# A spectral filter branch beside a split-fp16 feed-forward branch: first products and subtractions reordered, third quarter's rows in a place of their own, unit stores on GpSimd sooner, filter loaded for two quarters at a time

## The chip, the cores and the metric

One core of one Trainium2 chip. The metric is the device time of one execution in microseconds (us). The kernel before the change took 1266.6 us, the median of three runs (1266.14 to 1267.13).

## The reference

x has 2048 rows of 1024. Its rows are normalised, and two branches work on the result: a two-dimensional real Fourier transform, multiplied by a complex filter and transformed back, and a feed-forward network with hidden width 3584.

```python
def _A_ref(x, w_r, w_i):
    X = jnp.fft.rfft2(x, axes=(-2, -1))
    X = X * (w_r + 1j * w_i)
    return jnp.fft.irfft2(X, s=(S, D), axes=(-2, -1))

def _B_ref(x, w1, w2):
    h = _silu(jnp.einsum("bsd,df->bsf", x, w1))
    return jnp.einsum("bsf,fd->bsd", h, w2)

xn = _layernorm(x, axis=-1)
s = _A_ref(xn, A_w_r, A_w_i)
g = _silu(_B_ref(xn, B_w1, B_w2))
return x + s * g
```

## The kernel before

Every number of a product is held as a high and a low fp16 part, so that one product of 128x512 is three matmuls (high by high, high by low, low by high). DVE makes the low parts (`low`, L271, and L961 for the rows), ACT the high parts (`high`, L268, and L957).

**Order.** Nothing here is ordered by a scheduler. The kernel issues every engine's instructions itself: TensorE's products are a list, and behind each product a function (the one that ends with the loop over `bg` near L1705) takes a step of background work from the queues `bg` (normalisation, Fourier work), `wq` (weights), `xq`, `yq` and `sq` (sums of weights). Each piece is a generator, and a `yield` ends its step. A model of the clock decides how far DVE's work may run ahead of TensorE's (`LEAD`, 2.5 us). `defer(n, ...)` puts a load or store n steps later. Each engine takes its instructions strictly in the order issued, and an instruction that waits holds up all behind it. SP, ACT and POOL issue DMAs from the same order as their other work.

**Start.** The rows come in four quarters c of 512 rows, each of four row tiles p. `load_x` loads one row tile, `ln_gen(c)` normalises it: statistics on DVE (L936 to L939), the scale on POOL (L941 to L943), the normalisation on ACT (L944), and for c = 0 and 1 transposes on TensorE (`tp`, L953), whose results ACT and DVE split (L957, L961). Quarters 2 and 3 go through `turned`: ACT normalises into `xp` and writes the high part of `xs` (L922), DVE the low part (L915), and SP transposes both by DMA (L908). The row tiles of all quarters share four places; a row tile of the next quarter is loaded when its place comes free. `mm1(c, f)` is one product pa{c}_{f} of 24 matmuls (L618) for the hidden tile f of w1; DVE finds each w1 tile's scale (L303, L275 to L278). `spin` matmuls (L1716), counted by `WARM`, keep TensorE at work before the first product. fa0 to fa3 (L1017 to L1019) are the first Fourier stage; `AT` says behind which product of quarter 1 the first two of them stand. Each finished pair of hidden tiles gives sums and differences, split and stored to DRAM as "units" of seven blocks (`hosum`, `hoone`; stores at L702): the first two units through SP's queue, all others through POOL's.

**Middle.** Strassen-like products for the first half of the hidden width (L656), then the second matrix product in blocks pb{m}_{j} of 42 matmuls (L784 to L786), whose left operands `w<-hd` ACT's queue loads back from DRAM (L741), five steps ahead. w2's blocks, r, are loaded by SP (L556), some have a second block added by an accumulating DMA from POOL's queue (L561), and are split by ACT (L268) and DVE (L271).

**Filter stage.** Woven into that, `f_gen` goes through 16 units u: a second Fourier stage on TensorE (`fx`, L1234 to L1236) from vq (`load_v`, L1212), a radix-4 step on DVE that gives X (to L258), the multiplication by the filter (L1312, L1313), four sums into Z (L1341 to L1344), and the split of Z (ACT L1263, DVE L1273), of which each four units are stored to zd by POOL (L1256, the last high part from a tile called fs). `load_w(u)` loads the filter's real and imaginary parts for one unit, 128x4x128 fp32 each (L1220), and ACT scales them (L1298). `part_of(u)` gives unit u's group q and its column block j; for j = 0 POOL copies a column of X (L1294). X, T2 (the second product) and Z take turns in three places.

**Edge.** The column at the half frequency is worked out by `edge_gen` in small steps: copies on POOL (L1368 to L1371), nine small matmuls (eps, L1375 to L1377), ACT's copy (L1380), some thirty operations of 128x16 on POOL (L1385), a scaling (L1421), then ACT and DVE write zp (L1424, L1425). Its first step is taken in unit 13.

**Inverse.** `i_gen` reads zd back (SP, L1483), POOL copies a column of zp into it (L1574), and TensorE does the inverse transforms (iu L1499, id L1528).

Of the kernel before, what the change touches and what calls it, by code (L numbers as in the profile page):

```python
# [21 lines left out]
WARM = [35, 8, 0, 8, 0, 8, 12, 0, 0, 0]  # L22
# [8 lines left out]
AT = (1, 0)  # L31
# [111 lines left out]
def spectral_ffn(ctx, tc, x, w_r, w_i, w1, w2, ca, kc, ci, tw, pm, out):  # L143
# [467 lines left out]
    def mm1(c, f):  # L611
        ps = pf.tile([128, 512], F32, name=f"pa{c}_{f}", tag="ff")
        w, xt = w1t[f], xnT[c]
        terms = [(d, wh, xh) for wh, xh in ((0, 0), (0, 1), (1, 0)) for d in range(8)]
        if c + f:
            terms.sort(key=lambda k: k[0])
        for n, (d, wh, xh) in enumerate(terms):
            nc.tensor.matmul(ps, w[:, wh, d], xt[:, xh, d], start=(n == 0), stop=(n == 23))  # L618
        if c == 3:
            used1.add(f)  # L620
            done1.pop(f)()
        q, g = f // 2, c // 2

        def evac():
            if (q, g) not in h32:
                h32[q, g] = H["h"].tile([128, 4, 512], F32, name=f"h32_{q}_{g}", tag="h32", bufs=2)
            hq = h32[q, g]
            nc.scalar.activation(hq[:, 2 * (c % 2) + f % 2], ps, AF.Silu, scale=ep[:, q:q + 1])  # L628
            if c % 2 and f % 2:
                return hidden(q, g)  # L630

        return evac
# [259 lines left out]
    def load_x(c, p):  # L892
        tag, bufs = ("Ro", 1) if (c, p) == (0, 3) else ("x", 4)
        t_ = A["p"].tile([128, 1024], F32, name=f"x{c}_{p}", tag=tag, bufs=bufs)
        nc.sync.dma_start(t_, xs[4 * c + p])
        A["x"][c, p] = t_
# [4 lines left out]
    def turned(c, stats, norm):  # L901
# [9 lines left out]
        for i in range(4):  # L911
            if i >= 2:
                for p in (2 * i - 4, 2 * i - 3):
                    turn(p, 0)
                    nc.vector.tensor_tensor(split[:, p, 1], xn[p], split[:, p, 0], op=OP.subtract)  # L915
                    turn(p, 1)
            if i in (1, 2):
                for p in (2 * i - 2, 2 * i - 1):
                    xn[p] = ap.tile([128, 8, 128], F32, name=f"xp{c}_{p}", tag="Rs", bufs=2)
                    norm[p](xn[p].rearrange("s d1 d0 -> s d0 d1"), A["x"][c, p].rearrange("s (d0 d1) -> s d0 d1", d1=8))  # L920
                    A["x"].pop((c, p))
                    nc.scalar.activation(split[:, p, 0], xn[p], AF.Copy)  # L922
                    if c < 3:
                        defer(1, lambda p=p: load_x(c + 1, p))
            if i < 2:
                for p in (2 * i, 2 * i + 1):
                    stats(p)
            yield 2.5

    def ln_gen(c):  # L930
# [33 lines left out]
        if c == 0:  # L964
# [18 lines left out]
            hi(3)  # L983
            yield 0
            lo(2)
# [6 lines left out]
        for i in range(4):  # L992
            pair = range(2 * (i % 2), 2 * (i % 2) + 2)
            for p in pair:
                if i < 2:
                    stats(p)
                else:
                    trans(p)
                    if c < 3:
                        load_x(c + 1, p)  # L1000
# [187 lines left out]
    def open_f():  # L1188
        spots = {"K": (32, 38), "vq": (44, 48), "xc": (28,), "xb": (30,), "xd": (62,), "T1": (24,), "zl": (8,)}
        spots = {k: [(X1, v * KB) for v in vs] for k, vs in spots.items()}  # L1190
        spots["w"] = [(X1, 52 * KB + 2064 * k) for k in range(4)]
        spots["X"] = [(X1, 16 * KB), (X1, 20 * KB), (R2[0], 60 * KB)]
# [5 lines left out]
        load_w(1)  # L1198

    def part_of(u):  # L1200
        return u // 4, (u % 4 if u < 12 else (u - 1) % 4)
# [13 lines left out]
    def load_w(u):  # L1215
        q, j = part_of(u)
        n = 129 if j == 3 else 128
        for i in range(2):
            t_ = B["p"].tile([128, 4, n], F32, name=f"wq{u}_{i}", tag="w", bufs=4)
            nc.sync.dma_start(t_, wv[i][q][:, :, 128 * j:128 * j + n])  # L1220
            B["w"][u, i] = t_

    def f_gen():
# [21 lines left out]
        load_v(1)  # L1245
        yield PAUSE
# [33 lines left out]
        for u in range(16):  # L1280
# [9 lines left out]
            X = bp.tile([128, 8, 128], F32, name=f"X{u}", tag="X", bufs=3)  # L1290
# [4 lines left out]
            w_ = [B["w"].pop((u, i)) for i in range(2)]  # L1295
            for i in range(2):
                wf = w_[i].rearrange("m a k -> m (a k)")
                nc.scalar.activation(wf, wf, AF.Copy, scale=zs)  # L1298
                if j in (0, 3):
                    at = 0 if j == 0 else 128  # L1300
                    nc.scalar.activation(xsv[:, 1 + j // 3, q, :, i:i + 1], w_[i][:, :, at:at + 1], AF.Copy)
# [7 lines left out]
            wr, wi = (t_[:, :, 0:128].unsqueeze(2).broadcast_to([128, 4, 2, 128]) for t_ in w_)  # L1309
            t1 = bp.tile([128, 4, 2, 128], F32, name=f"T1{u}", tag="T1", bufs=1)  # L1310
            t2 = bp.tile([128, 4, 2, 128], F32, name=f"T2{u}", tag="X", bufs=3)
            tt(t1, Xv, wr, op=OP.mult)  # L1312
            tt(t2, Xv, wi, op=OP.mult)  # L1313
            if u + 2 < 16:
                defer(2, lambda u=u: load_w(u + 2))
# [4 lines left out]
            if u >= 13:  # L1320
# [11 lines left out]
            if u >= 14:  # L1332
# [4 lines left out]
            Z = bp.tile([128, 8, 8, 16], F32, name=f"Z{u}", tag="X", bufs=3)  # L1337
# [131 lines left out]
    def open_r2():  # L1469
        R2[0] = A["r2"].enter_context(tc.tile_pool(name="r2", bufs=1, side="right")).tile([128, 19520], F32, name="r2")  # L1470
# [199 lines left out]
    with tc.manual_schedule():  # L1670
# [27 lines left out]
        def work():  # L1698
# [5 lines left out]
            for _ in range(3):  # L1704
                if clock["dve"] > clock["pe"] + LEAD or hold[0] or slot(bg) == PAUSE:  # L1705
# [25 lines left out]
        for k, q in enumerate((bg, wq, bg, wq, bg, wq, wq, bg, wq)):  # L1731
            slot(q)
            spin(WARM[1 + k])
        for i in range(4):
            load_x(1, i)
            if i == 1:
                load_fwd()
        for c in range(1, 4):
# [5 lines left out]
        order = [(c, f) for fs in ((0, 1, 2, 3), (4, 5)) for c in range(2) for f in fs]  # L1744
        order += [(c, f + i) for f in (0, 2, 4) for c in (2, 3) for i in range(2)]
        order += [(c, f + i) for f in range(6, 2 * NPL, 2) for c in range(4) for i in range(2)]
        t_job = None
        for n, (c, f) in enumerate(order):
            if f == 0 and c:
                finish(bg, ln[c])  # L1750
            if ln[3].done and stores[0] is nc.sync:
                stores[0] = nc.gpsimd
# [167 lines left out]
```

## Time and profile before

| | |
|---|---|
| Median of three runs | 1266.6 us |
| The profiled execution, its own time | 1267.57 us |
| Its span in the profile | 1265.8 us |
| Mean granted TensorE clock | 0.995 |
| Busy: PE, DVE, ACT, POOL | 1232.4, 991.6, 567.0, 272.5 us |
| DMA | 306.68 MB, mean 242 GB/s |

The span leaves out 1.77 us around it. All times below that have a start are microseconds from the span's start. "<-" behind a wait names what ended it; a row "x16" stands for 16 instructions one behind the other, with the time that they took together.

### The profile page before, as it was taken

The numbers are of one execution on the slowest core, as the hardware profiler recorded it, in microseconds if no ns is written. First come the engines' busy times: TensorE is split into PE (matmuls) and PEld (weight loads), VectorE is DVE, ScalarE is ACT, GpSimd is POOL, SyncE is SP. The second block draws the span as 40 slices with busy tenths as digits, with TensorE's granted clock in tenths as the row PEclk, the third lists the DMA queues.
The fourth block names the chain that finished last, engine by engine and source line by source line (L and its number), as shares of the span: only waits on it lengthen the run. The fifth ranks groups of instructions, "written<-read, shape, count | busy, mean of one in ns | idle before, by whom it ended". The sixth has DMA issues, their size and how long they took to land. (4 is left out here: it accounts for less than half of the span.)

```text
span 1265.8 us, 18607 instructions
## 1 busy us (share of the span) xinstructions
PE 1232.4 (97%) x6827; PEld 639.3 (51%) x6827; DVE 991.6 (78%) x1646; ACT 567.0 (45%) x844; POOL 272.5 (22%) x428
## 2 busy tenths in 40 slices
PE   8999999999999999999999999999999989999998
PEld 5544444444444444444545455555554446666654
DVE  6677998889996977897587869996799238977875
ACT  4755465755457777766423223232333113412221
POOL 1321243433242313342200000202121400110111
PEclk9999999999999999999999999999999999999999
DMA  7469697767569878866956788989999998987687
GB/s 235 127 155 234 159 305 220 221 185 220 118 186 254 245 241 281 247 194 217 333 152 201 243 253 212 314 251 279 221 299 290 320 344 281 341 279 277 220 268 270
DMA packets 184187, 306.68 MB, mean 242 GB/s; under 512 B 32032, under 2 KB 92448, under 8 KB 182944
## 3 DMA queue, kind: packets, MB, share of 16 engines
q1 hardware_dynamic: 138176, 163.85, 42.8%
q0 software_dynamic: 30128, 92.82, 25.5%
q10 hardware_dynamic: 15792, 48.83, 10.9%
q8 instruction: 53, 0.87, 0.3%
q14 instruction: 38, 0.31, 0.1%
HBM read 204.25 MB, written 111.67 MB: 250 GB/s over the span
## 5 line engine op out<-in xcount | busy, mean ns | idle before, releaser
L618 PE MATMUL pa<-xn,w 128*128 128x512 f16 x1536 | 335.5, 380 | 6.8 <-DMA xn<-xs 2.4
L784 PE MATMUL pb<-r,w 128*128 128x512 f16 (+1 forms) x798 | 299.5, 375 | 1.7 <-DMA w<-hd_one 1.7
L785 PE MATMUL pb<-r,w 128*128 128x512 f16 (+1 forms) x798 | 299.5, 375 | 0.0
L786 PE MATMUL pb<-r,w 128*128 128x512 f16 (+1 forms) x798 | 299.5, 375 | 0.0
L618 PEld LDWEIGHTS <-w 128*128 128x128 f16 x1536 | 150.2, 98 | 188.1 <-issue 4.2
L656 PEld LDWEIGHTS <-w 128*128 128x128 f16 x1008 | 98.5, 98 | 124.8 <-issue 5.5
L786 PEld LDWEIGHTS <-w 128*128 128x128 f16 x798 | 78.1, 98 | 91.2
L784 PEld LDWEIGHTS <-w 128*128 128x128 f16 x798 | 78.1, 98 | 88.3 <-DMA w<-hd_one 3.2
L785 PEld LDWEIGHTS <-w 128*128 128x128 f16 x798 | 78.1, 98 | 85.0
L656 PE MATMUL pa<-r,w 128*128 128x512 f16 x432 | 99.1, 379 | 4.8 <-ACT pc L668 2.6
L268 ACT ACTIVATE r<-r,sc 128x512 f16<-128x512 f32 x88 | 61.1, 715 | 93.0 <-DMA r<-in_B_w_dram 66.0
L271 DVE SCALAR_TENSOR_TENSOR r<-r,sc 128x512 f16<-128x512 f32 x88 | 65.0, 747 | 38.0 <-ACT r L268 38.0
L702 POOL DMA_DIRECT2D hd_one<-hoone x52 | 45.7, 879 | 178.2 <-DVE hoone L271 158.2
L271 DVE SCALAR_TENSOR_TENSOR hoone<-h,hs,hoone 128x2048 f16<-128x2048 f32 x28 | 65.7, 2346 | 8.1 <-ACT hoone L268 7.9
L268 ACT ACTIVATE hoone<-h,hs 128x2048 f16<-128x2048 f32 x28 | 55.8, 1994 | 14.1 <-DMA hd_one<-hoone 8.0
L702 POOL DMA_DIRECT2D hd_sum_d<-hosum x26 | 23.6, 907 | 165.3 <-DVE hosum L271 107.9
L268 ACT ACTIVATE hosum<-hr,hs 128x1536 f16<-128x1536 f32 x28 | 43.9, 1568 | 34.1 <-DVE hr L709 23.4
L271 DVE SCALAR_TENSOR_TENSOR hosum<-hr,hs,hosum 128x1536 f16<-128x1536 f32 x28 | 50.7, 1812 | 9.3 <-ACT hosum L268 9.3
L628 ACT ACTIVATE h<-pa,ep 128x512 f32<-128x512 f32 x64 | 43.2, 677 | 32.7 <-PE pa L618 30.7
L1499 PE MATMUL iu<-xn 128*128 128x256 f16 x384 | 44.6, 273 | 4.7 <-POOL xn L1574 2.6
L1234 PE MATMUL fx<-xn 128*128 128x256 f16 x192 | 44.8, 279 | 4.0 <-DVE r L271 2.9
L708 DVE TENSOR_TENSOR hr<-h 128x1024 f32<-128x1024 f32 x28 | 34.2, 1220 | 14.3 <-ACT h L628 13.1
(292 smaller groups left out, 2060.2 us busy)
## 6 DMA issues: line engine op xcount, KB each, us to landing
w<-hd_dif ACTq DMA_DIRECT2D x32, 448.0 KB, 7.0
r<-in_B_w_dram SPq DMA_DIRECT2D x56, 256.0 KB, 8.0
w<-hd_sum ACTq DMA_DIRECT2D x32, 448.0 KB, 6.6
w<-hd_one ACTq DMA_DIRECT2D x32, 448.0 KB, 7.3
hd_sum<-hosum POOLq DMA_DIRECT2D x52, 256.0 KB, 6.0
hd_one<-hoone POOLq DMA_DIRECT2D x52, 256.0 KB, 4.7
hd_dif<-hoone POOLq DMA_DIRECT2D x52, 256.0 KB, 4.4
xn<-in_B_w_dram SPq DMA_DIRECT2D x40, 256.0 KB, 4.9
```

Source lines behind the costliest of these rows:

```text
L268: nc.scalar.activation(hi, raw, AF.Copy, scale=scale)
L271: nc.vector.scalar_tensor_tensor(lo, raw, scale, hi, op0=OP.mult, op1=OP.subtract)
L618: nc.tensor.matmul(ps, w[:, wh, d], xt[:, xh, d], start=(n == 0), stop=(n == 23))
L628: nc.scalar.activation(hq[:, 2 * (c % 2) + f % 2], ps, AF.Silu, scale=ep[:, q:q + 1])
L656: nc.tensor.matmul(ps, lhs(d, wh), rhs(d, xh), start=(name in ("M1", "M5") and d + n == 0), stop=(d + n == 5), skip_group_check=True)
L702: defer(1, lambda k=k, m=m: stores[0].dma_start(hd[m, g][:, :, q].rearrange("f p h s -> f p (h s)"), o[:, k].rearrange("f p h s -> f p (h ...
L708: tt(sums[:, 0:2], hq[:, 0::2], hq[:, 1::2], op=OP.subtract)
L784: nc.tensor.matmul(ps, hh[:, 0], w[:, 0], start=first, stop=False)
L785: nc.tensor.matmul(ps, hh[:, 0], w[:, 1], start=False, stop=False)
L786: nc.tensor.matmul(ps, hh[:, 1], w[:, 0], start=False, stop=last)
L1234: nc.tensor.matmul(o, k[:, c, kh, 1], v[:, c, vh], start=(n == 0), stop=False)
L1499: nc.tensor.matmul(ps[:, q], lhs, rhs, start=(n == 0 and r == 0), stop=(n == 2 and r == 1))
```

## The change

Seven things are edited.

1. In `ln_gen(0)` the third row tile's subtraction is issued one step sooner, two slots of the start change places, and `WARM` changes with them.
2. `mm1` for c >= 1 takes its terms in the order high-high, low weight, low row; pa1_0 takes them one whole group behind the other. pa1_0 goes ahead of fa0_0 and fa0_1 (`AT`), and pa1_4 ahead of pa0_5.
3. The row tiles of quarter 2 get places of their own and are loaded at the start, behind those of quarter 1; those of quarter 3 are loaded from `ln_gen(1)`.
4. `LEAD` is 6 between the issue of w1's sixth tile and the end of quarter 3's normalisation.
5. The units' stores go to POOL's queue from the second step of quarter 3's normalisation on, so that all units go there.
6. `load_w(t)` loads the filter for two units at once, 128x4x256 (or 257), in four places; ACT scales them at once. T2 overwrites X, X and Z take turns in two places. Units 12 to 15 take the column blocks 0, 1, 3, 2 instead of 3, 0, 1, 2.
7. `edge_gen`'s first step is taken in unit 14, a second one per unit from unit 15.

```diff
 NP = NFT // 2
-WARM = [35, 8, 0, 8, 0, 8, 12, 0, 0, 0]
+WARM = [35, 8, 0, 8, 0, 2, 16, 0, 0, 0]
 LEAD, PAUSE, EARLY = 2.5, -1, 2
...
 TURNED = (2, 3)
-AT = (1, 0)
+AT = (1, 1)
 EXTRA = (4, 5, 6, 7, 20, 22, 24)
...
         w, xt = w1t[f], xnT[c]
-        terms = [(d, wh, xh) for wh, xh in ((0, 0), (0, 1), (1, 0)) for d in range(8)]
-        if c + f:
+        terms = [(d, wh, xh) for wh, xh in (((0, 0), (1, 0), (0, 1)) if c else ((0, 0), (0, 1), (1, 0))) for d in range(8)]
+        if (c, f) not in ((0, 0), (1, 0)):
             terms.sort(key=lambda k: k[0])
...
         tag, bufs = ("Ro", 1) if (c, p) == (0, 3) else ("x", 4)
-        t_ = A["p"].tile([128, 1024], F32, name=f"x{c}_{p}", tag=tag, bufs=bufs)
+        if c == 2:
+            t_ = view(X1, 48 * KB + 4 * KB * p, [128, 1024], F32)
+        else:
+            t_ = A["p"].tile([128, 1024], F32, name=f"x{c}_{p}", tag=tag, bufs=bufs)
         nc.sync.dma_start(t_, xs[4 * c + p])
...
                     nc.scalar.activation(split[:, p, 0], xn[p], AF.Copy)
-                    if c < 3:
-                        defer(1, lambda p=p: load_x(c + 1, p))
             if i < 2:
...
                     stats(p)
+            if c == 3 and i == 1:
+                stores[0] = nc.gpsimd
             yield 2.5
...
             hi(3)
-            yield 0
             lo(2)
+            yield 0
             lo(3)
...
                     trans(p)
-                    if c < 3:
-                        load_x(c + 1, p)
+                    load_x(3, p)
             if i < 2:
...
         spots = {k: [(X1, v * KB) for v in vs] for k, vs in spots.items()}
-        spots["w"] = [(X1, 52 * KB + 2064 * k) for k in range(4)]
-        spots["X"] = [(X1, 16 * KB), (X1, 20 * KB), (R2[0], 60 * KB)]
+        spots["w"] = [(X1, 52 * KB), (X1, 56 * KB), (R2[0], 60 * KB), (R2[0], 72 * KB + 256)]
+        spots["X"] = [(X1, 16 * KB), (X1, 20 * KB)]
         spots["zh"] = [(X1, 0), (H["scr"], 0)]
...
         load_w(0)
-        load_w(1)
 
     def part_of(u):
-        return u // 4, (u % 4 if u < 12 else (u - 1) % 4)
+        return u // 4, (u % 4 if u < 12 else (0, 1, 3, 2)[u % 4])
 
...
 
-    def load_w(u):
-        q, j = part_of(u)
-        n = 129 if j == 3 else 128
+    def load_w(t):
+        q, j = t // 2, 2 * (t % 2)
+        n = 257 if j else 256
         for i in range(2):
-            t_ = B["p"].tile([128, 4, n], F32, name=f"wq{u}_{i}", tag="w", bufs=4)
+            t_ = B["p"].tile([128, 4, n], F32, name=f"wq{t}_{i}", tag="w", bufs=4)
             nc.sync.dma_start(t_, wv[i][q][:, :, 128 * j:128 * j + n])
-            B["w"][u, i] = t_
+            B["w"][t, i] = t_
 
...
         load_v(1)
+        load_w(1)
         yield PAUSE
...
             tt(d.rearrange("m c r k -> m c (r k)"), pv[:, 0:2], cpy, op=OP.subtract)
-            X = bp.tile([128, 8, 128], F32, name=f"X{u}", tag="X", bufs=3)
+            X = bp.tile([128, 8, 128], F32, name=f"X{u}", tag="X", bufs=2)
             radix4(-1, b, d, X)
...
                 nc.gpsimd.tensor_copy(xsv[:, 0, q], Xv[:, :, :, 0])
-            w_ = [B["w"].pop((u, i)) for i in range(2)]
-            for i in range(2):
+            w_ = [B["w"][u // 2, i] for i in range(2)]
+            for i in range(2 if u % 2 == 0 else 0):
                 wf = w_[i].rearrange("m a k -> m (a k)")
                 nc.scalar.activation(wf, wf, AF.Copy, scale=zs)
-                if j in (0, 3):
-                    at = 0 if j == 0 else 128
-                    nc.scalar.activation(xsv[:, 1 + j // 3, q, :, i:i + 1], w_[i][:, :, at:at + 1], AF.Copy)
+                at = 256 if u % 4 else 0
+                nc.scalar.activation(xsv[:, 2 if at else 1, q, :, i:i + 1], w_[i][:, :, at:at + 1], AF.Copy)
             yield 2.8
...
                 high_z(u - 1)
-            wr, wi = (t_[:, :, 0:128].unsqueeze(2).broadcast_to([128, 4, 2, 128]) for t_ in w_)
+            wr, wi = (t_[:, :, 128 * (j % 2):128 * (j % 2) + 128].unsqueeze(2).broadcast_to([128, 4, 2, 128]) for t_ in w_)
             t1 = bp.tile([128, 4, 2, 128], F32, name=f"T1{u}", tag="T1", bufs=1)
-            t2 = bp.tile([128, 4, 2, 128], F32, name=f"T2{u}", tag="X", bufs=3)
+            t2 = Xv
             tt(t1, Xv, wr, op=OP.mult)
             tt(t2, Xv, wi, op=OP.mult)
-            if u + 2 < 16:
-                defer(2, lambda u=u: load_w(u + 2))
+            if u % 2 and u < 13:
+                defer(2, lambda u=u: load_w(u // 2 + 2))
             if u == 12:
...
                 edge = edge_gen()
-            if u >= 13:
+            if u >= 14:
                 next(edge, None)
...
                 low_z(u - 1)
-            if u >= 14:
+            if u >= 15:
                 next(edge, None)
...
                 copy(u + 1)
-            Z = bp.tile([128, 8, 8, 16], F32, name=f"Z{u}", tag="X", bufs=3)
+            Z = bp.tile([128, 8, 8, 16], F32, name=f"Z{u}", tag="X", bufs=2)
             bv = b2.rearrange("m a r (i l) -> m a r l i", l=8)
...
             for _ in range(3):
-                if clock["dve"] > clock["pe"] + LEAD or hold[0] or slot(bg) == PAUSE:
+                if clock["dve"] > clock["pe"] + (LEAD if ln[3].done or 5 not in w1t else 6) or hold[0] or slot(bg) == PAUSE:
                     break
...
         spin(WARM[0])
-        for k, q in enumerate((bg, wq, bg, wq, bg, wq, wq, bg, wq)):
+        for k, q in enumerate((bg, wq, bg, wq, bg, wq, bg, wq, wq)):
             slot(q)
...
                 load_fwd()
+        for i in range(4):
+            load_x(2, i)
         for c in range(1, 4):
...
 
-        order = [(c, f) for fs in ((0, 1, 2, 3), (4, 5)) for c in range(2) for f in fs]
+        order = [(c, f) for c in range(2) for f in range(4)] + [(c, f) for f in (4, 5) for c in range(2)]
         order += [(c, f + i) for f in (0, 2, 4) for c in (2, 3) for i in range(2)]
         order += [(c, f + i) for f in range(6, 2 * NPL, 2) for c in range(4) for i in range(2)]
-        t_job = None
+        t_job = sum_job = None
         for n, (c, f) in enumerate(order):
...
                 finish(bg, ln[c])
-            if ln[3].done and stores[0] is nc.sync:
-                stores[0] = nc.gpsimd
+            if ln[3].done and not sum_job:
                 sum_job = add(sq, sum_gen())
```

In the following rows a name such as w_67 is a tile that is used again and again, tp_2 is the transposed third row tile, and r_, xn stand for big regions. From the row loads (L894) on, the kernel after has its lines shifted by one to three.

DVE at the start, before, from the first w1 tile's second maximum on (L303 maxima, L275 to L278 its scale, L961 low parts of the rows, L271 low parts of w1):

```order
L303 TENSOR_REDUCE m_221<-w_67 128x1
L275 TENSOR_SCALAR ep<-s_0_402 128x1
L276 TENSOR_SCALAR ep<-ep 128x1
L277 RECIPROCAL rs_225<-ep 128x1
L278 TENSOR_SCALAR hs<-rs_225 128x1
L271 SCALAR_TENSOR_TENSOR w_67<-w_67,rs_225 128x1024
L961 TENSOR_TENSOR xn<-tp_2_362,xn 128x8x128
L961 TENSOR_TENSOR xn<-tp_3_383,xn 128x8x128
L271 SCALAR_TENSOR_TENSOR w_67<-w_67,rs_225 128x1024
```

The same stretch after (L964 is the former L961):

```order
L303 TENSOR_REDUCE m_221<-w_67 128x1
L964 TENSOR_TENSOR xn<-tp_2_362,xn 128x8x128
L275 TENSOR_SCALAR ep<-s_0_397 128x1
L276 TENSOR_SCALAR ep<-ep 128x1
L277 RECIPROCAL rs_225<-ep 128x1
L278 TENSOR_SCALAR hs<-rs_225 128x1
L964 TENSOR_TENSOR xn<-tp_3_383,xn 128x8x128
L271 SCALAR_TENSOR_TENSOR w_67<-w_67,rs_225 128x1024 x2
```

One of the two low parts now stands ahead of the scale, the other ahead of the first of w1's low parts.

POOL at the end of the filter stage, before (L1385 "ISA" stands ahead of the edge's operations; L561 accumulating loads of w2, L1256 stores of zd):

```order
L561 DMA r_2501<-in_B_w_dram 128x512 x7
L1385 ISA
L1385 TENSOR_TENSOR xn<-xsv,xn 128x16 x3
L1385 TENSOR_TENSOR xn<-xn,xsv 128x16
L1385 TENSOR_TENSOR xn<-xsv,xn 128x16 x4
L1385 TENSOR_TENSOR xn<-xn 128x16 x14
L561 DMA r_2501<-in_B_w_dram 128x512 x4
L1256 DMA zd<-fs 128x4096
L561 DMA r_2501<-in_B_w_dram 128x512
L1256 DMA zd<-xn 128x4096
L1385 TENSOR_TENSOR xn<-xn 128x16 x2
L1385 TENSOR_TENSOR xn<-xn 128x4 x8
```

And after (L1258 and L1386 are the former L1256 and L1385):

```order
L561 DMA r_2496<-in_B_w_dram 128x512 x10
L1258 DMA zd<-fs 128x4096
L561 DMA r_2496<-in_B_w_dram 128x512
L1258 DMA zd<-xn 128x4096
L1386 ISA
L1386 TENSOR_TENSOR xn<-xsv,xn 128x16 x3
L1386 TENSOR_TENSOR xn<-xn,xsv 128x16
L1386 TENSOR_TENSOR xn<-xsv,xn 128x16 x4
L1386 TENSOR_TENSOR xn<-xn 128x16 x16
L1386 TENSOR_TENSOR xn<-xn 128x4 x8
L1422 TENSOR_SCALAR xn<-xn 128x32
```

The whole edge now stands behind the last accumulating load and both stores of zd.

ACT at the same place, before (L741 loads of w from hd, L865 an activation of a finished block):

```order
L268 ACTIVATE r_2501<-r_2501,sc_229 128x512
L741 DMA w_67<-hd_one_1_94 128x1792
L268 ACTIVATE r_2501<-r_2501,sc_229 128x512
L1424 ACTIVATE zp<-xn 128x16x2
L741 DMA w_67<-hd_one_1_94 128x1792
L865 ACTIVATE pl_2_1_8559<-pl_2_1_8559,c_228 128x512
L268 ACTIVATE r_2501<-r_2501,sc_229 128x512 x2
L741 DMA w_67<-hd_one_1_94 128x1792 x2
L865 ACTIVATE pl_3_1_8632<-pl_3_1_8632,c_228 128x512
```

And after (L1425 is the former L1424):

```order
L268 ACTIVATE r_2496<-r_2496,sc_229 128x512
L741 DMA w_67<-hd_one_1_94 128x1792
L268 ACTIVATE r_2496<-r_2496,sc_229 128x512
L741 DMA w_67<-hd_one_1_94 128x1792
L865 ACTIVATE pl_2_1_8499<-pl_2_1_8499,c_228 128x512
L268 ACTIVATE r_2496<-r_2496,sc_229 128x512
L1425 ACTIVATE zp<-xn 128x16x2
L268 ACTIVATE r_2496<-r_2496,sc_229 128x512
L741 DMA w_67<-hd_one_1_94 128x1792 x2
L865 ACTIVATE pl_3_1_8572<-pl_3_1_8572,c_228 128x512
```

ACT's write of zp now stands behind one more load of w and ahead of the next two.

On TensorE the products keep their order but for pa1_0 and pa1_4 (above); the edge's nine matmuls stood ahead of pb4_0 and now stand behind pb4_1.

More of the change, by code (lines that the diff above doesn't have):

```diff
@@ L1469, in open_r2 @@
     def open_r2():
[L1470 removed]
+        R2[0] = A["r2"].enter_context(tc.tile_pool(name="r2", bufs=1, side="right")).tile([128, 19524], F32, name="r2")
     def open_fd():
```

2 lines of the change are left out of this document (1 added, 1 removed).

## The prediction

> **What bounds the kernel now.** I read the page first, then TensorE's waits, then a table of stretches, then the timelines of the engines that those waits name. The page's first lines:
>
> ```profile
> span 1265.8 us, 18607 instructions
> PE 1232.4 (97%) x6827; PEld 639.3 (51%) x6827; DVE 991.6 (78%) x1646; ACT 567.0 (45%) x844; POOL 272.5 (22%) x428
> ```
>
> TensorE is busy 97% of the span: only 1265.8 - 1232.4 = 33 us can be won by fewer waits, besides what the clock loses. The change takes 2 spin matmuls away and no product. So each part is judged by the waits it touches. TensorE's waits (line, what it waited for, us in all, times, longest):
>
> ```profile
> PE iu L1499 <- POOL xn L1574: 2.6, 1, 2.6
> PE pa L618 <- DMA xn<-xs: 2.4, 2, 1.3
> PE pa L618 <- DVE w L271: 2.2, 1, 2.2
> PE pb L784 <- DMA w<-hd_one: 1.7, 3, 1.3
> PE pa L618 <- DVE xn L961: 1.7, 1, 1.7
> PE fa L1017 <- DVE xn L961: 1.5, 1, 1.5
> ```
>
> These six, 12.1 us, lie where the change works; two more, of fx, stand below. Behind some waits the granted clock also fell. The stretches (length, then PE's, PEld's, DVE's, ACT's, POOL's busy time, granted clock, DMA share, GB/s):
>
> ```profile
> 100.00:120.00 20.00, 17.61 (x74) 7.38 (x73) 17.49 (x30) 11.12 (x12) 0.20 (x1) 0.91 0.90 223
> 890.00:925.00 35.00, 30.95 (x195) 17.34 (x193) 27.41 (x48) 10.39 (x22) 3.42 (x4) 0.95 0.98 259
> 1000.00:1046.00 46.00, 39.54 (x228) 21.51 (x226) 15.59 (x28) 9.51 (x14) 0.26 (x1) 1.00 0.95 347
> ```
>
> Work at 0.91 for 17.61 us loses 1.6, at 0.95 for 30.95 us loses 1.5. From 890 to 925 and from 1000 to 1046 the DMA engines are 95% busy and more: a load there waits for others.
>
> **Start.** DVE, TensorE's first product behind it, and ACT's last high rows of quarter 1:
>
> ```profile
> 17.72 0.16 DVE L275 TENSOR_SCALAR ep<-s 128x1 int32<-128x1 int32 x1 [1.40 <-PE s L283]
> 19.48 1.28 DVE L271 SCALAR_TENSOR_TENSOR w<-w,rs 128x1024 f16<-128x1024 f32 x1 [1.03 <-ACT w L268]
> 20.69 2.35 DVE L961 TENSOR_TENSOR xn<-tp,xn 128x1024 f16<-128x1024 f32 x2
> 23.09 3.61 PE L618 MATMUL pa<-xn,w 128*128 128x512 f16 x16 [1.68 <-DVE xn L961]
> 45.30 1.94 ACT L957 ACTIVATE xn<-tp 128x1024 f16<-128x1024 f32 x2 [3.30 <-PE tp L953]
> ```
>
> Each L961 takes 2.35/2 = 1.18. The first fits into the 1.40 that DVE waits ahead of the scale, the second nearly into the 1.03 ahead of L271. The low rows are then there about 20, before TensorE's first eight matmuls end: -1.7. pa1_0 begins with high rows only, where fa waited 1.5 for low ones. ACT has the high ones at 47.24, DVE's last low ones take another half of a pair's 2.35 or less: between nothing and -1.1, I take -0.4. So TensorE is 2.1 ahead when it comes to pa0_4, and there a new wait opens:
>
> ```profile
> 65.39 1.23 DVE L915 TENSOR_TENSOR xs<-xp,xs 128x1024 f16<-128x1024 f32 x1 [1.93 <-ACT xs L922]
> 70.04 1.28 DVE L271 SCALAR_TENSOR_TENSOR w<-w,rs 128x1024 f16<-128x1024 f32 x1
> 50.31 26.50 PE L618 MATMUL pa<-xn,w 128*128 128x512 f16 x122
> 79.02 15.28 PE L618 MATMUL pa<-xn,w 128*128 128x512 f16 x70 [2.21 <-DVE w L271]
> ```
>
> A matmul is 26.50/122 = 0.217. pa0_4 is the fifth product from 50.31: its third matmul, the first with w_4's low part, stood at 50.31 + 98 x 0.217 = 71.6, and that part was ready at 71.3. Coming 2.1 earlier it waits up to 1.8. DVE's chain to it begins with a wait for ACT's xs, which the earlier rows shorten; I grant 0.3 and take +1.5. pa0_5's 2.2 goes, because pa1_4 (24 x 0.217 = 5.2 us) now stands ahead of it: -2.2. Next, quarter 3's rows (first row ACT, second SP):
>
> ```profile
> 94.73 2.00 ACT L268 ACTIVATE hoone<-h,hs 128x2048 f16<-128x2048 f32 x1 [5.36 <-DMA hd_one<-hoone]
> 94.65 12.12 SPq L908 DMA_TRANSPOSE xn<-xs  x8
> ```
>
> ACT waited 5.36 for the first unit's store before it could go on to quarter 3's third row tile, and SP's eight transposes stretched over 12.12 us behind ACT and DVE. In the new order xp and xs stand ahead of that hoone, and SP has no unit stores between: I expect the last transpose some us ahead of TensorE, so -2.4 for its two waits and -1.6 for the clock. What comes next is the copy of pa1_4's result on ACT, now behind the xs work and a hoone whose store is on POOL:
>
> ```profile
> L702 POOL DMA_DIRECT2D hd_one<-hoone x52 | 45.7, 879 | 178.2 <-DVE hoone L271 158.2
> ```
>
> POOL's stores take 0.88 us each to issue, seven of them 6.2, so TensorE may wait for a bank; I bound that by nothing and half of it, 3.1, and take 1.2. Start: -1.7 - 0.4 + 1.5 - 2.2 - 2.4 - 1.6 + 1.2 = **-5.6**, between -7.5 and -3. I expect it to stay won, since the helpers behind it are released by TensorE itself and come earlier with it.
>
> **Filter.** The two fx waits end with the landing of a vq tile:
>
> ```profile
> 891.92 1.58 SPq L1212 DMA_DIRECT2D xn<-vd  x1
> 907.70 0.27 PE L1234 MATMUL fx<-xn 128*128 128x256 f16 x1 [2.86 <-DVE r L271]
> 909.93 0.55 SPq L1212 DMA_DIRECT2D xn<-vd  x1
> 922.41 0.27 PE L1234 MATMUL fx<-xn 128*128 128x256 f16 x1 [1.19 <-DMA xn<-vd]
> ```
>
> 907.70 - 891.92 = 15.8 and 922.41 - 909.93 = 12.5 us from issue, so although the first is put down to DVE, I read both as vq. What the wider loads give back is seen in SP's queue from 740 to 960 (packets, MB, share of 16 engines):
>
> ```profile
> q1 hardware_dynamic: 23327, 27.81, 51.0%
> L1220 SPq DMA_DIRECT2D xn<-in_A_w_r_dram x14: 368/426/1813, 749.0 to 942.1; - x14
> ```
>
> 51.0% of 220 us is 112 us. The filter has 14 loads there of its real part (second row) and as many of the imaginary, of 128x4 rows each: 28 x 512 = 14,336 packets of 512 bytes or a little more, 61% of that queue's packets and 26% of its bytes. If time goes by packets, halving them saves 112 x 0.61 / 2 = 34 us of a saturated queue, more than the two waits need; if by bytes, nothing. The Trainium skill ("DMA: Bandwidth & Descriptors", "Why small descriptors are slow (HBM only)") gives three cycles a packet beside one per 32 bytes; by it 19 cycles twice become 35 once, 8% of the filter's time, and this term would be about 0. The cost of a packet by itself isn't in the trace, so I go between: of 2.86 + 1.19 and the clock's 1.5 I take **-3.4**, between 0 and -5.6. T2 over X, fewer ACT scalings and the later second load I cost at nothing: DVE makes X, T2 and Z in one order anyhow, and a filter pair has four units' time.
>
> **Edge.** POOL, then ACT, SP, TensorE:
>
> ```profile
> 979.76 2.55 POOL L1385 TENSOR_TENSOR xn<-xsv,xn 128x16 f32<-128x16 f32 x3 [8.84 <-ACT pl L865]
> 986.43 3.75 POOL L561 DMA_DIRECT2D r<-in_B_w_dram  x4
> 996.00 0.56 POOL L1256 DMA_DIRECT2D zd<-xn  x1 [1.45 <-PE pb L786]
> 996.58 1.61 POOL L1385 TENSOR_TENSOR xn<-xn 128x16 f32<-128x16 f32 x10
> 990.93 0.72 ACT L268 ACTIVATE r<-r,sc 128x512 f16<-128x512 f32 x1 [11.90 <-DMA r<-in_B_w_dram]
> 1004.05 1.01 ACTq L741 DMA_DIRECT2D w<-hd_one  x2
> 1011.59 0.92 SPq L1483 DMA_DIRECT2D xn<-zd  x2
> 1011.62 0.39 PE L784 MATMUL pb<-r,w 128*128 128x512 f16 x1 [0.16 <-DMA w<-hd_one]
> 1025.77 0.26 POOL L1574 COPY xn<-zp 128x16 f16<-128x16 f16 x1 [27.14 <-DMA xn<-zd]
> ```
>
> Before, 8.84 us ahead of the first L1385 (the "ISA" row of the order) and 986.43 - 979.76 = 6.7 of its work held four accumulating loads back; ACT stood 11.90 for them, so that w's loads came late (1.7 us of waits), and the last zd store stood at 996.0, so that its reading back ended at 1025.77 (2.6). Those go: -4.3. But all of the edge now follows that store. I put the store at 990 (996.0 less half the 11.9). Then 6 to 8.84 for the ISA (part of the 8.84 may be the wait that the row names), and 6.7 + 1.6 of work: the edge ends at 1004.3 to 1007.1, and the two loads behind it on ACT are issued about 1 later, at 1005.3 to 1008.1. Before, that load took 1011.62 - 1004.05 = 7.6, so it lands 1012.9 to 1015.7, where TensorE would come at 1011.62 - 1.7 = 1009.9: +3.0 to +5.8, and I take +5.3, because the full 8.84 is what the trace shows. Net **+1.0**; with the store at 984 none is added (-4.3), with the store at 996 about +8.
>
> **Sum.** -5.6 - 3.4 + 1.0 = -8.0: the profiled 1267.57 becomes 1259.6. The median is 0.97 below the profiled run, so 1258.6.
>
> **Rivals.**
>
> *The filter's packets give nothing.* The bytes stay, the DMA share stays at 0.98, and both fx waits stay. For it: 15.8 us for one vq tile is queueing behind others' bytes as well as packets. Time: 1258.6 + 3.4 = 1262. The page named above would have it so. Chance 0.20.
>
> *The start gives less*: pa0_4's wait and the late bank take what the rest brings, -3 in place of -5.6, with one of the other terms poorer: 1261 to 1264, counted with the first; together 0.28.
>
> *Everything is kept*: -7.5 - 5.6 - 4.3 = -17.4, 1249.2. It needs zd's store at 984 and the vq loads 3 us faster. Chance of under 1255: 0.16.
>
> *The edge is late*: store at 996, +8 in place of +1: 1265.6, no change. For it: POOL still takes eleven loads, one by one, ahead of that store. Chance 0.13.
>
> *Slower: the copy on POOL in unit 12.* X is now overwritten by T2, so DVE's second multiply waits for POOL's copy of X's column, and the new column order puts that copy into unit 12, behind eleven accumulating loads, each of which waits for its DMA:
>
> ```profile
> 906.80 0.85 POOL L561 DMA_DIRECT2D r<-in_B_w_dram  x1 [14.70 <-DMA r<-in_B_w_dram]
> 909.04 1.72 POOL L561 DMA_DIRECT2D r<-in_B_w_dram  x2 [1.39 <-DMA r<-in_B_w_dram]
> ```
>
> The last of these ended at 910.8, and unit 12's second multiply would come at about 918 or, with fx's waits gone, 914. From there on each us that the last load is late holds DVE, and TensorE behind its r. A second wait like the 14.70 would cost 14.7 - 3 to 7 = 8 to 11.5, and 1.5 of clock; the filter's gain would be gone: 1258.6 + 3.4 + 9.5 to 13 = 1271.5 to 1275. Against it: the margin of 3 to 7 us. Chance 0.06; with the edge at its worst and a poor start, slower in all 0.08.
>
> **How the numbers follow.** Forecast, 1255 to 1261: 0.35; under it 0.16; 1261 to 1264: 0.28; no change 0.13; slower 0.08. A run of this kernel tells 0.2%, 2.5 us, from no change: faster is under 1264.1, 0.79. The range 1251 to 1267 leaves out some 0.08 below and 0.11 above.
>
> **What would show it.** Right: in the profile after, the first L618 wait is gone; a DVE wait of 1 to 2 us stands at pa0_4; no wait for xs and a clock of 1.00 from 100 to 120; fx waits under 2 us in all; ACT standing at L1425 for POOL, and a wait for w<-hd_one of 3 to 6 us behind it, none for L1574. Wrong: if TensorE waits for xs still, if DVE stands at the second multiply for POOL, or if POOL's edge ends before 1000.

## The result: slower by 0.6%, and the profile after

The changed kernel took 1274.2 us, the median of five runs (1272.2 to 1279.7), beside 1267.1 for the kernel before. The ratio is 1.0059, 95% interval 1.0033 to 1.0084: **7.5 us slower**, where 8 faster was forecast. The profiled execution was the fastest of the five, 1272.16 us. Its page begins:

```profile
span 1270.4 us, 18562 instructions
PE 1231.8 (97%) x6825; PEld 638.7 (50%) x6825; DVE 992.0 (78%) x1646; ACT 562.6 (44%) x828; POOL 278.3 (22%) x442
```

TensorE's busy time is the same, so the loss is waiting. Its waits after (line, what it waited for, us in all, times, longest):

```profile
PE pa L618 <- DMA xn<-xs: 9.3, 2, 5.4
PE iu L1500 <- POOL xn L1575: 4.9, 1, 4.9
PE pa L618 <- ACT h L628: 1.7, 1, 1.7
PE pa L618 <- DVE w L271: 1.6, 1, 1.6
PE pb L784 <- DMA w<-hd_one: 1.6, 1, 1.6
PE fx L1235 <- DMA xn<-vd: 0.9, 1, 0.9
```

The wait for xs, quarter 3's transposed rows, was 2.4 and is 9.3. The two fx waits of 2.9 and 1.2 are gone (the 0.9 left is another, at the second of the 16 units). The stretches, with the columns as before the change:

```profile
100.00:120.00 20.00, 10.68 (x42) 4.23 (x40) 15.01 (x34) 4.85 (x5) 5.41 (x9) 0.74 0.94 185
890.00:925.00 35.00, 35.00 (x213) 18.54 (x212) 32.50 (x54) 12.27 (x24) 4.79 (x6) 1.00 0.95 287
1000.00:1046.00 46.00, 39.55 (x207) 21.09 (x205) 13.44 (x25) 7.59 (x12) 6.42 (x34) 0.93 0.91 332
```

From 100 to 120 us TensorE works 10.7 of 20 us and at 0.74 of its clock; from 890 to 925 it now works throughout. To see where time came from and went, I compare when TensorE begins the same piece of work. Start times in us, read from TensorE's timelines (the experiments' kernels are told below; the profiled executions of e1 and e3 were the slowest of their twelve, 1269.2 and 1269.9 us beside medians of 1264.1 and 1267.1):

| First matmul of | before | after | e1 | e12 | e3 | e4 | e9 |
|---|---|---|---|---|---|---|---|
| fa0_2, ahead of pa2_0 | 94.14 | 90.63 | 90.82 | 90.73 | 94.25 | 95.95 | 90.59 |
| next fa, behind quarter 3's first products | 120.62 | 125.95 | 118.18 | 114.66 | 120.64 | 118.75 | 115.22 |
| first fx (filter stage) | 741.43 | 748.76 | 742.52 | 738.87 | 743.73 | 741.60 | 739.72 |
| fx of unit 13 | 922.41 | 924.79 | 922.86 | 916.72 | 920.81 | 925.48 | 915.59 |
| first iu (inverse stage) | 1026.08 | 1030.16 | 1027.58 | 1023.16 | 1028.28 | 1029.72 | 1016.14 |

After against before, row by row: -3.5; then +8.8 in the second stretch; +2.0 in the long middle (620.8 before, 622.8 after; e3 and e4, which leave the start alone, take 623.1 and 622.9, so that is not the change); -5.0 in the filter stage; +1.7 at the edge. A row by itself tells little below 2 us: e3 and e4 have the start of the kernel before, and differ from it by up to 1.9 us in the first two rows. All of the loss is made between fa0_2 and the next fa, 26 us long before and 35 after. There SP's transposes of quarter 3 and GpSimd's stores stand like this, then TensorE's two waits:

```profile
88.08 0.71 POOL L702 DMA_DIRECT2D hd_one<-hoone x1 [6.08 <-DVE hoone L271]
98.71 0.71 POOL L702 DMA_DIRECT2D hd_sum_d<-hosum x1 [7.71 <-ACT hoone L268]
102.96 1.03 POOL L702 DMA_DIRECT2D hd_one<-hoone x1
```

```profile
108.30 1.01 PE L618 MATMUL pa<-xn,w 128*128 128x512 f16 x2 [3.94 <-DMA xn<-xs]
114.69 10.56 PE L618 MATMUL pa<-xn,w 128*128 128x512 f16 x42 [5.39 <-DMA xn<-xs]
```

The first unit's last four stores are issued from 88.08 on, the second unit's seven from 98.71 to 104. DVE had the last low part of xs at 96.4; its transpose was issued at 101.9 and landed at 114.7. The time from a transpose's issue to its landing, after and then before (shortest, median, longest):

```profile
DMA to landing us min/median/max: 3.0/4.2/12.7
```

```profile
DMA to landing us min/median/max: 3.2/3.3/5.8
```

12.7 us where 5.8 was the longest. The DMA queues tell why this can be: before, from 94.6 to 107 us and then from 98 to 106 alone, and after, from 88 to 97 (queue, packets, MB, share of 16 engines):

```profile
q1 hardware_dynamic: 8924, 2.55, 98.4%
```

```profile
q1 hardware_dynamic: 6365, 1.58, 103.7%
```

```profile
q1 hardware_dynamic: 2408, 0.60, 44.9%
q0 software_dynamic: 320, 1.05, 44.7%
```

Before, SP's queue alone kept the 16 DMA engines 98% busy through the eight transposes. The first window still has 1290 packets of 512 bytes of the stores ahead of them; the second has the transposes alone, in packets of at most 256 bytes, and they fill the engines by themselves, at 1.58 MB in 8 us, 198 GB/s (the share passes 100% because a packet's whole time is booked where it starts). After, GpSimd's stores took 44.7% of the engines beside them, and the transposes moved 0.60 MB in 9 us.

### The profile page after: what moved, and what is told of

It reads as the page before. It is cut to its first block, busy times and chain, and to the rows that moved or that the text cites. A ratio compares the mean times of both kernels' runs of the same rounds, so it can differ in the third digit from the quotient of the medians.

```text
span 1270.4 us, 18562 instructions
## 1 busy us (share of the span) xinstructions
PE 1231.8 (97%) x6825; PEld 638.7 (50%) x6825; DVE 992.0 (78%) x1646; ACT 562.6 (44%) x828; POOL 278.3 (22%) x442
## 5 line engine op out<-in xcount | busy, mean ns | idle before, releaser
L702 POOL DMA_DIRECT2D hd_one<-hoone x56 | 53.1, 948 | 178.8 <-DVE hoone L271 149.7
L271 DVE SCALAR_TENSOR_TENSOR r<-r,sc 128x512 f16<-128x512 f32 x88 | 64.9, 746 | 20.5 <-ACT r L268 15.1
L271 DVE SCALAR_TENSOR_TENSOR hoone<-h,hs,hoone 128x2048 f16<-128x2048 f32 x28 | 65.7, 2345 | 9.2 <-ACT hoone L268 9.1
L271 DVE SCALAR_TENSOR_TENSOR hosum<-hr,hs,hosum 128x1536 f16<-128x1536 f32 x28 | 50.7, 1812 | 8.9 <-ACT hosum L268 8.9
L702 POOL DMA_DIRECT2D hd_sum<-hosum x56 | 47.7, 1019 | 0.1
```

The costliest lines, as they stand in the source:

```text
L271: nc.vector.scalar_tensor_tensor(lo, raw, scale, hi, op0=OP.mult, op1=OP.subtract)
L702: defer(1, lambda k=k, m=m: stores[0].dma_start(hd[m, g][:, :, q].rearrange("f p h s -> f p (h s)"), o[:, k].rearrange("f p h s -> f p (h ...
```

## The experiments

Twelve kernels ran, each beside the kernel before on the same chip. Theories A to C and their successors O, P, Q and S are named where they were put down. Ratios are to the kernel before, with the 95% interval.

### e1 and e2: the stores' queue

e1 undoes the change of queue alone, e2 makes that change alone in the kernel before:

```diff
-            if c == 3 and i == 1:
-                stores[0] = nc.gpsimd
...
             if ln[3].done and not sum_job:
+                stores[0] = nc.gpsimd
                 sum_job = add(sq, sum_gen())
```

> The changed kernel with its first two units' stores on SP's queue again. Theory A (stores on GpSimd's queue share the DMA engines with SP's transposes of quarter 3 and hold these up: the last landed 12.7 us after its issue where before it was 3.3): the two waits for xs fall from 9.3 us to under 3, the clock from 100 to 120 us is near 1.0, and the kernel takes 1262 to 1266 us. Theory B (xs itself is late because of the new order on ACT and DVE, the queue does not matter): the waits stay at 7 to 10 us, 1272 to 1275 us. Theory C (in SP's own queue the stores again stand ahead of the transposes and hold them as long): waits 4 to 7 us, 1267 to 1270 us.

> The kernel before with only the first two units' stores moved to GpSimd's queue. Theory A: its transposes are slowed as well, the waits for xs grow from 2.4 to 6 to 10 us, 1272 to 1276 us. Theories B and C: the transposes have SP's queue to themselves and come sooner, waits of 0 to 2.4 us, 1264 to 1267 us.

e1: ratio 0.9971 (0.9957 to 0.9986), 3.7 us faster than before and 11 faster than the changed kernel. e2: 1.0030 (1.0014 to 1.0046), 3.8 slower. e1's clock from 100 to 120 us is 0.91, as before, and not the 1.0 expected. TensorE's waits for xs in e1, then in e2, and e2's stretch:

```profile
PE pa L618 <- DMA xn<-xs: 2.7, 1, 2.7
```

```profile
PE pa L618 <- DMA xn<-xs: 5.0, 2, 4.3
100.00:120.00 20.00, 14.73 (x57) 5.91 (x56) 13.57 (x19) 10.76 (x10) 2.92 (x4) 0.83 0.80 203
```

Theory A holds both ways: the stores' move is the loss, in either kernel. e2's wait is a little under the 6 us expected, and its price smaller than in the changed kernel: there four of the second unit's stores are issued only from 111.56 on, behind the transposes. Part of e2's wait goes by way of ACT, which now stands 9.0 us for the first unit's store where it stood 5.4, so that quarter 3's third row tile comes 4 us later. B is out. C, that SP's queue would hold the transposes as long, is out for the time; e1's wait of 2.7 shows that something of it is there.

### e5 and e12: queue, packets or order

That left the mechanism open. e5 issues the first two units' stores from ACT (`stores[0] = nc.scalar` at the same place), whose queue sends 512-byte packets. e12 leaves them on GpSimd's queue, and lets the second unit's wait there until the transposes have landed:

```diff
+                late = 3 if (q, g) == (1, 0) else 1
+                if late == 3 and n == 3:
+                    defer(3, lambda: nc.gpsimd.tensor_copy(small("seen"), xnT[3][:, 1, 0, 511:512]))
                 for k, m in sorted(enumerate(names), key=lambda t: t[1] != "sum_d"):
-                    defer(1, lambda k=k, m=m: stores[0].dma_start(
+                    defer(late, lambda k=k, m=m: stores[0].dma_start(
```

> The changed kernel with the first two units' stores issued by ACT: a second hardware queue beside SP's transposes, whose store packets are 512 bytes where GpSimd's were 4096. Theory P (the DMA engines take a packet from each queue in turn, so each 256-byte packet of a transpose waits for one of the other queue's, 18 against some 250 ns): with packets of 29 ns the transposes issue in 1.3 to 2 us and land within 3.3 to 6 us. Theory S (any second queue in parallel slows them, by bytes): the last ones land 8 to 13 us after issue, as in the changed kernel. ACT now waits for DVE at each store, so the time is no measure of P: 1264 to 1272 us under P, 1272 or more under S.

> The changed kernel, all units' stores still on GpSimd's queue, but the second unit's seven wait there until quarter 3's transposes have landed. Theory O (order: the transposes keep all DMA engines busy by themselves, and every store that runs beside them comes on top; SP's queue had half of the second unit's behind them): only the first unit's last four stores still run beside them, the last transpose lands within 4 to 6 us of its issue, the waits for xs fall from 9.3 to 1 to 4 us, 1264 to 1268 us. Theory Q (GpSimd's queue itself, its 4096-byte packets or its slower issue): a wait of 4 us or more for xs stays, and ACT's wait for the later stores is added, 1271 to 1276 us.

e5: 0.9962 (0.9948 to 0.9977). No wait for xs, longest landing 6.2 us. That is about as P said, but it does not show P: ACT is in order, and came to the second unit's stores only at 100.23, when the transposes had been issued. The first unit's last four stores, 1.05 MB beside the transposes in both, do not tell the queues apart either. The fifth of quarter 3's transposes was issued at 96.96 with GpSimd's stores and at 95.52 with ACT's, but with ACT's its row tile came 2 us later (94.06 in place of 92.04). In e1, where the same four stores stood ahead of the transposes in SP's queue, it was issued at 96.95: beside them or ahead of them, these four delay it alike. What differs is the second unit's seven.

e12 decides. The wait of GpSimd, its next stores, then the transposes' landing and TensorE's stretch:

```profile
104.30 0.72 POOL L703 CAST seen<-xn 128x1 f32<-128x1 f16 x1 [13.20 <-DMA xn<-xs]
104.97 0.71 POOL L705 DMA_DIRECT2D hd_sum_d<-hosum x1
```

```profile
DMA to landing us min/median/max: 3.0/3.3/7.5
```

```profile
100.00:120.00 20.00, 20.00 (x112) 9.85 (x111) 16.93 (x34) 6.50 (x9) 7.99 (x11) 1.00 0.96 275
```

The same stores on the same queue in the same packets, only behind the transposes: the last transpose lands by 104.3 in place of 114.7, TensorE has no wait for xs, and the clock is 1.00. The ratio is 0.9953 (0.9937 to 0.9969), 6.0 us faster than before, 13 faster than the changed kernel. Theory O holds (with no wait for xs where 1 to 4 us were expected, and a longest landing of 7.5 where 4 to 6 were), and Q falls: the same queue does no harm when its stores run behind.

Two things stay open. Whether GpSimd's 4096-byte packets cost more beside the transposes than ACT's of 512 bytes was not tested with the same stores at the same time. And the bytes alone do not make up the loss: from 109 to 114 us in the changed kernel, with the last transposes still out, all queues together moved 0.46 MB, 93 GB/s, where the transposes alone ran at 198. What held the engines there is not shown.

### e7 and e8: the other parts of the start

e7 is the kernel before with the reordered subtractions and products alone (`WARM`, the slots, `lo(2)`, the terms of `mm1`, `AT`, `order`), e8 is e1 with the rows' loads as they were before.

> The kernel before with only the reordered first subtractions and products. If TensorE's gain to the 94th us (3.4 us in the changed kernel's trace) comes from these: 1.5 to 3.5 us gained by there; then the transposes of quarter 3, which do not come sooner, take some of it back: waits for xs of 3 to 5.5 us, 1265 to 1268 us. If the rows of quarter 2 in their own place are needed for it: no gain by the 94th us.

> The changed kernel with the two units' stores back on SP and quarter 2's and 3's rows loaded as before. If the own place is what lets quarter 3's transposes start sooner: they start 3 to 5 us later than with it, the waits for xs grow from 2.7 to 4 to 7 us, 1266 to 1269 us. If it does nothing: within 1 us of the first experiment, 1263 to 1265 us.

e7: 0.9997 (0.9983 to 1.0011), no difference. fa0_2 begins at 90.71, so the whole 3.4 us come from the reordering; by the next fa (120.22) they are given back to the transposes, which start only 1.6 us sooner:

```profile
PE pa L618 <- DMA xn<-xs: 4.2, 2, 2.8
```

e8: 0.9971 (0.9955 to 0.9987), the same as e1. The transposes begin at 90.63 us, in e1 at 90.45: the own place does nothing here. It was expected to bring 3 to 5 us. What does bring them sooner is edit 4: of all edits to the start, e7 and e8 differ in `LEAD` alone, and quarter 3's transposes begin at 93.04 in e7 and the wait for xs is 4.2, in e8 1.8. What `LEAD` is worth in time was not run by itself.

### e3, e4 and e6: filter and edge

e3 is the kernel before with the filter's and the edge's part of the change, e4 with the edge's alone (`u >= 14` and `u >= 15`).

> The kernel before with only the filter loads for two units and the later edge. If the wider loads are what took the fx waits of units 12 and 13 and the low clock away (about -6 us in the traces, against +2 of the edge): 1262 to 1264 us, no fx wait over 1 us. If they went only because TensorE came 8 us later to that stage: the fx waits of 2.9 and 1.2 us stay, and with the edge it is 1267 to 1270 us.

> The kernel before with only the edge's first step in unit 14, its second per unit from unit 15. If the edge's place costs what the traces show (ACT stands at the write of zp, then SP's load of kc waits for the edge's place): the wait of iu grows from 2.6 to 4 to 6 us, and 1268 to 1271 us. If the four accumulating loads it lets through are worth as much: 1265 to 1267 us.

e3: 0.9983 (0.9968 to 0.9998), 2.2 faster. e4: 1.0014 (0.9999 to 1.0028), 1.8 slower. So the filter's edit as a whole (two units at a time; the "two quarters" of the title are a slip) is worth about 3.9 us (0.0031 of 1267; by the two intervals, between 1 and 7), with the start untouched.

That is less than expected: e3's 1267.1 lies in the band of the rival theory, and one fx wait of 2.0 stays. But that theory, in which the waits go only because TensorE comes later, is out. From the first fx to unit 13 the five kernels with the old loads (before, e2, e4, e7, e11) take 181.0 to 183.9 us, with 4.1 to 6.8 us of fx waits; the nine with the new ones take 175.0 to 180.3, with 0 to 3.4, and e8, e9 and e12 come to that stage earlier than the kernel before.

The packets show in SP's queue, 220 us of the filter stage in the changed kernel:

```profile
q1 hardware_dynamic: 16214, 28.62, 47.0%
```

47.0% where it was 51.0%: with some 7,000 packets fewer the queue takes 0.04 x 220 = 9 us less of all engines, with more bytes moved. The packets in the traces have a price of their own: the median is 27 ns at 512 bytes and 46 at 1024, so one of 1024 saves 8 ns against two of 512, and 7,000 save 3.5 us of 16 engines. The rest of the 9 us is not explained. That the packets, and not T2's place, the fewer scalings or the new order of the units, make the gain is argued and not shown: e3 has them all.

The edge costs about what was expected of it, though e4's interval just reaches no change: from unit 13's fx to the first iu the three kernels with the old edge (before, e2, e7) take 100.4 to 104.2 us, seven with the later one 104.2 to 108.8. In the changed kernel ACT and SP wait for it like this:

```profile
1009.48 0.23 ACT L1425 ACTIVATE zp<-xn 128x32 f16<-128x32 f32 x1 [11.64 <-POOL xn L1422]
```

```profile
SPq L1482 <- DVE zp L1426: 11.1, 1, 11.1
```

SP stands 11.1 us at the load of kc, whose place the edge still holds, and behind it stands the reading back of zd. e6 is e1 with that order turned round for the first column group:

```diff
-        nc.sync.dma_start(k, kc[c])
+        if c != IORDER[0]:
+            nc.sync.dma_start(k, kc[c])
...
         if c == IORDER[0]:
+            defer(1, lambda: nc.sync.dma_start(k, kc[c]))
```

> The changed kernel with the two units' stores back on SP and, at the entry of the inverse stage, zd read back ahead of kc. If SP standing at the load of kc for the edge's place (11 us in the changed kernel's trace) is what makes iu wait: that wait falls from 5 to 0 to 2 us, 1259 to 1262 us. If zd's own stores or the full DMA engines are: it stays at 4 to 6 us, 1263 to 1266 us.

e6: 0.9969 (0.9955 to 0.9984), no gain on e1. The wait of iu is gone, and another has its place:

```profile
PE pb L784 <- DMA w<-hd_one: 9.2, 1, 9.2
```

zd was read from 1000.8 on, ahead of w, while ACT still stood 12.6 us for the edge with w's loads behind it. SP's order does make iu wait, as told, but it is not what costs the time: the edge itself was late, and one wait was traded for the other.

### e9 to e11: the gap ahead of the edge

What makes the edge late, then? In the changed kernel GpSimd sits idle for 7.39 us between zd's last store and the edge's first addition:

```profile
1002.71 0.59 POOL L1386 TENSOR_TENSOR xn<-xsv,xn 128x16 f32<-128x16 f32 x3 [7.39 <-issue]
```

It is where the order shows the "ISA" row. One small addition at the start of the filter stage, where GpSimd waits anyhow, moves that row there:

```diff
         mat(0)
+        nc.gpsimd.tensor_tensor(small("early"), mhalf, mhalf, op=OP.add)
         yield 1
```

e9 is e1 with it, e10 the same with the two units' stores on ACT (as e5), e11 the kernel before with it.

> The changed kernel with the two units' stores back on SP and one small addition on GpSimd at the start of the filter stage, where GpSimd stands idle, so that the 7 to 9 us ahead of the edge's first addition fall there. If those are what makes ACT's write of zp, w's loads and the reading back of zd late: ACT's wait at zp falls from 11.6 to under 5 us, the waits for w and for iu from 5 to 10 us together to 0 to 3, 1257 to 1261 us. If the full DMA engines set these waits: they move but keep their sum, as in the sixth experiment, 1262 to 1265 us.

> The same small addition, with the first two units' stores issued by ACT. If both work as told: no wait for xs and none for iu over 1 us, 1256 to 1260 us, faster than every other version. If not: 1262 to 1265 us.

> The kernel before with that small addition alone. There the 8.8 us held back four accumulating loads, ACT's 11.9 us and zd's last store. If they set the waits at the entry of the inverse stage (1.7 us for w, 2.6 for iu): these fall to under 1 us in all, 1263 to 1266 us. If not: no difference, 1267 to 1269 us.

e9: 0.9916 (0.9897 to 0.9936), 10.7 us faster than before, where e1 was 3.7. e10: 0.9908 (0.9884 to 0.9932), no different from e9, though it was expected to be the fastest of all: e9's wait for xs of 1.9 is gone, and one of 2.4 for ACT's copy of a result stands in its place. e11: 0.9969 (0.9955 to 0.9984), 3.9 faster. In e9 the idle time stands at 739.70, 9.44 us that nobody waits for, the edge follows zd's store at once, and ACT waits 3.5:

```profile
739.70 0.18 POOL L1278 TENSOR_TENSOR early<-mhalf 128x1 f32<-128x1 f32 x1 [9.44 <-issue]
986.50 0.85 POOL L1256 DMA_DIRECT2D zd<-xn x1
987.07 0.89 POOL L1385 TENSOR_TENSOR xn<-xsv,xn 128x16 f32<-128x16 f32 x3
```

```profile
994.13 0.23 ACT L1424 ACTIVATE zp<-xn 128x32 f16<-128x32 f32 x1 [3.49 <-POOL xn L1421]
```

In e9, pb's wait for w is 0.3 and iu's for GpSimd's copy 1.3. In e11 iu's is still 2.2 where under 1 was expected, but w's is gone. From unit 13's fx to the first iu, e9 and e10 take 100.6 and 98.6 us, where the seven with the later edge and without that addition took 104.2 to 108.8. e9 and e10 are the fastest versions of this study; neither was combined with e12's order.

## Why the prediction was wrong, point by point

**What failed** is one step of the start: "SP has no unit stores between: I expect the last transpose some us ahead of TensorE, so -2.4 for its two waits and -1.6 for the clock." I took a queue of its own for a road of its own, and put what the moved bytes would do to the transposes at nothing. The two waits did not go: they grew from 2.4 to 9.3, and the clock fell from 0.91 to 0.74. The transposes already filled the 16 DMA engines by themselves, as the trace of before could tell (103.7% from 98 to 106 us; 0.90 DMA share in the quoted row from 100 to 120), and stores from another queue run on the same engines (44.7% beside 44.9% after the change). With its neighbour (+1.2 for a bank; the wait for h was 1.7) the step was to give -2.8 and gave +8.8 in the traces.

e1, e2 and e12 show the cause: that the stores, above all the second unit's seven, run beside the transposes, and not which engine issued them. The Trainium skill ("DMA: Bandwidth & Descriptors", "Issuing engines are not separate DMA queues") says that DMAs run on the same 16 engines and interleave whichever engine issued them, and that spreading them saves only issue time. The trace agrees, with the two shares above; here spreading them cost 11 us (e1 against the changed kernel), and I had not weighed the rule. My bound for the store's move looked at GpSimd's issue time and a bank, and not at what the bytes would meet.

**The rest of the start was right**: -1.7, -0.4, +1.5 and -2.2 make -2.8 up to fa0_2; the trace shows -3.5, e7 alone -3.4. The new wait for w's low part was expected at 1.5 and is 1.6. That part by itself is worth nothing (e7): what TensorE gains it loses at the transposes, which it meets earlier.

**What the start wins or loses stays**, as forecast: the changed kernel is 5.3 us behind in the second row of the table and 7.3 at the first fx, and the 2 us between are those that e3 and e4 also take.

**Filter: size right within the noise, mechanism likely.** -3.4 was forecast, e3 less e4 gives -3.9. The fx waits and the low clock of 890 to 925 us went. The prediction said that the cost of a packet isn't in the trace; it is, as 27 and 46 ns at 512 and 1024 bytes, and makes two become one 15% cheaper. By the Trainium skill's three cycles a packet ("DMA: Bandwidth & Descriptors", "Why small descriptors are slow (HBM only)") it is an estimated 8%, 2 to 6 us of the filter's 29 to 68, which I had called about 0; here the measurement decides. The rival that both fx waits stay fell.

**Edge: right in sum by luck, wrong in both waits.** +1.0 was forecast, +1.7 measured in the trace, +1.8 in e4. But I let iu's 2.6 go, because zd would be read back sooner. It became 4.9: SP reads kc first, and that load waits for the edge's place, a dependence that I had not looked for. The w wait was forecast at 5.3 (the full 8.84 us that I named as the reason give 5.8) and was 1.6: the edge ended later than I had it (1009.4, with zd's last store at 994.5 and not 990), but the load behind it landed in 3.8 us and not in the 7.6 of before. The two errors cancelled. That the "ISA" gap could be had for nothing elsewhere was in front of me: I priced it at 8.84 us and did not ask whether it must stand there.

**The slower rival** named the wrong place. GpSimd's copy in unit 12 held nobody: DVE's second multiply waited 0.4 us for it at most.

## What to carry to other kernels

When a transfer moves to another queue, look at the DMA engines' share in the stretch where it will now run, not at the queue. If the engines are full there with what the bound engine waits for, the transfer belongs behind it, in whichever queue (13 us between the changed kernel and e12). When an engine sits idle ahead of its first operation of another kind, try that operation once in an earlier pause. And a wait removed where an engine further back is still late only changes its name (e6).

## What the hardware showed that I had not expected

Eight DMA transposes, 2 MB, keep all 16 DMA engines busy for some 11 us, an estimate from the 6365 packets that took 103.7% of 8 us, and run at 198 GB/s. In the traces of before and after, a packet's median time on SP's queue was 18 ns at 256 bytes (the transposes), 27 at 512, 46 at 1024, 84 at 2048 and 159 at 4096: these fit some 9 ns for each packet beside its bytes, an estimate by which a transpose's packets spend half their time on it.

GpSimd stood idle ahead of its first addition behind its partition reductions, wherever that addition stood: 8.84 us in the kernel before, 7.39 after, 9.44 in e9, 9.61 in e10 and 11.90 in e11. In the last three it cost nothing. How much of each is needed and how much is a pause that was there anyhow, the profile does not say.
